# Forming the sums of quarters on GpSimd during the scan steps and storing them, in a kernel of attention and Fourier mixing

## The chip, the core and the metric

The kernel runs on one core of a Trainium2 chip. The metric is the device time of one execution in microseconds. Engines are called by their names: TensorE (PE; its weight loads are PEld), VectorE (DVE), ScalarE (ACT), GpSimd (POOL) and SyncE (SP), which here only issues transfers.

## The reference

```python
x = A_x                                          # 1 x 2048 x 512
g = sigmoid((x * gate_w).sum(-1, keepdims=True))
# a: attention, 32 heads of 16, 2048 queries and keys, softmax, then @ wo
# b: y = dft_seq_re @ (x @ dft_hid_re.T) - dft_seq_im @ (x @ dft_hid_im.T)
return g * a + (1 - g) * b
```

All is float32. The kernel splits each operand of a matmul whose rounding would show into a high part (fp32r) and the rest, and sums three products (high x high, high x low, low x high).

## The kernel before, in words

The work is one long program in an order written out by hand (`tc.manual_schedule()`): every engine has its own stream, in the order in which the Python code emits instructions, and an instruction waits on semaphores for what it needs. SP too takes its transfers in that order. In the built program most of SP's transfers also wait for the one eight places before them in its queue.

The front part projects queries, keys and values, forms the two spectral operands a and b (b is kept in DRAM as `b_d`), multiplies most of the sequence transform (all 16 row blocks of the real part, 0 to 5 of the imaginary part), and scans most of the scores for their row maxima beside it.

Then comes the main loop over `NP * PERIODS` = 512 steps: 16 pairs of heads, 32 steps each (2 halves of the queries by 16 blocks of keys). A half of a pair, 16 steps, is called half pair below. In each step TensorE forms scores (`qk_both`, `qk_single`, L228), ScalarE takes their exponential (L252, L260), and TensorE multiplies with the values (`pv`, L774). At the end of a half pair VectorE copies the sums out (`quotients`, L783), GpSimd spreads the denominators by small transfers (L786), ten steps later `divide` takes reciprocals on VectorE (L792) and lets GpSimd multiply, split and store (L793 to L810).

What stands beside it changes with the step:

- Steps 2 to about 317, the steps with scans: `next_scan` forms one more score block and VectorE reduces it to a maximum (L155).
- From step MIX = 317 on, `fill` gives TensorE six more matmuls in every step: first two row blocks of the spectral part (`spectral`), then, from step HALVED = 349 to 460, the half products (`crosses`), then the output projection (`mix_heads`, `mix_some`). In this part values are multiplied in every second step, for two steps together, so that the pattern repeats every two steps.

The half products replace the last 8 row blocks (rows 1024 to 2047) of the imaginary part, by symmetry. `CROSSES` lists seven products, each of 16 steps. An operand of a product has left parts (2 column blocks f by 2 units u, from `b_d`) and right parts (8 units u, from `ct`). Each is a quarter of its matrix, named (a, b), or a sum or difference of two quarters. `crossed` says at which step, counted from the product's start, each part is formed: from 8 steps before to 7 after. `crossing(r)` calls `begin_unit` (loads the quarters, L948 and L951) 4 steps before, and `form_unit` (L956) on the step: VectorE sums two quarters where there are two (L960), rounds to the high part (L963), and subtracts (L964). The loads go into the ring `craw` of 8 buffers. `gather` takes each finished half product out of the one pair of banks (`pair_banks`) with a copy and an add on VectorE (L1009, L1010), then GpSimd combines it.

The rows that a pair's scores need are loaded on SP: `load_use` for the pair in use (from its 18th step, for the next pair; spread over the steps from MIX on), `load_scan` for a pair to be scanned, and the shifts of the maxima are stored with L190. `load_y` brings in 4 row blocks of the spectral part in one transfer, two of them at step OUT - 25 = 436 and two at step 480. `load_turned` and `output_operands` use the ring `craw` later.

Of the kernel before, what the change touches and what calls it, by code (L numbers as in the profile page):

```python
# [10 lines left out]
F32 = mybir.dt.float32  # L11
# [7 lines left out]
P = 128  # L19
S = 2048  # L20
D = 512
H = 32
DH = 16
NP = H // 2
# [7 lines left out]
PERIODS = 2 * NB  # L32
# [18 lines left out]
OUT = MIX + NB * LATER - SAVED  # L51
# [5 lines left out]
CROSSES = [([((0, 0), 1), ((0, 1), 1)], [((1, 1), 1)]),  # L57
# [6 lines left out]


def build(tc, xT, wqkv, wo, wrT, wiT, cr, ci, ct, gate, out):
    nc = tc.nc
    with ExitStack() as ctx:
        keep = ctx.enter_context(tc.tile_pool(name="keep", bufs=1))
        stk = ctx.enter_context(tc.tile_pool(name="stk", bufs=6))  # L70
# [3 lines left out]
        dram = ctx.enter_context(tc.tile_pool(name="dram", bufs=1, space=DRAM))  # L74
# [7 lines left out]
        b_d = [dram.tile([4, P, D], F32, name=f"b_d{n}") for n in range(NB // 4)]  # L82
# [3 lines left out]
        y_d = [dram.tile([P, 4, D], F32, name=f"y_d{c}") for c in range(NC)]  # L86
# [36 lines left out]
        def load_use(p, spread=False):  # L123
            if p < NP:
                used[p], loads = row_loads(p, nc.sync)
                for load in loads:
                    load()
                    if spread:
                        yield
                qs, ks = used[p]  # L130
                for j in range(2):
                    b = 64 * j + 48
                    nc.sync.dma_start(ks[b:b + 2, :].bitcast(F32), ones_d)
                    for n in range(2):
                        nc.sync.dma_start(qs[b + n:b + n + 1, :].bitcast(F32),
                                          m_d[p][n:n + 1, :, j].rearrange("n g b k -> n b g k"))
# [68 lines left out]
        def block(i):  # L205
            return big.tile([P, 512], F32R, tag=f"b{i}", name=f"b{i}")
# [62 lines left out]
        with ExitStack() as pf:  # L269
# [100 lines left out]
            craw, ready = {}, {}  # L370
# [26 lines left out]
            with ExitStack() as px:  # L397
# [60 lines left out]
                kept = []  # L458
# [68 lines left out]
                raws = [stk.tile([P, S], F32, tag="stk", name="raws") for _ in range(6)]  # L527
# [123 lines left out]
            with ExitStack() as py:  # L651
# [36 lines left out]
                for n, (ph, t, u) in enumerate(coef):  # L688
# [12 lines left out]
                    hi, lo = ready.pop(n)  # L701
# [21 lines left out]
                    for w in range(CS):  # L723
                        s = u * CS + w
# [24 lines left out]
        with ExitStack() as pa:  # L749
            pr = pa.enter_context(tc.tile_pool(name="pr", bufs=1, reuse_waits="tile"))  # L750
            cw = pa.enter_context(tc.tile_pool(name="cw2", bufs=2, reuse_waits="tile"))
            ap = pa.enter_context(tc.tile_pool(name="ap", bufs=1, reuse_waits="tile"))
# [63 lines left out]
            ys, oc = {}, {}  # L816
# [64 lines left out]
                                nc.sync.dma_start(a[i][64 * c + j:64 * c + 64:4, :].bitcast(F32), src[0:DH, j])  # L881
                direct[h].append(a)

            def load_y(c):
                y4 = stk.tile([P, 4, D], F32, tag="stk", name="y4")
                nc.sync.dma_start(y4, y_d[c])
                for t in range(4 * c, 4 * c + 4):
                    ys[t] = y4[:, t % 4, :]

            def take_in(t, ps):  # L890
                nc.vector.scalar_tensor_tensor(ys[t], ps, g[:, t:t + 1], ys[t], op0=ALU.mult, op1=ALU.add)
# [2 lines left out]
            raws, units = [], [(t, u) for t in range(NB - LATER, NB - CROSS) for u in range(NU)]  # L894
            parts = []

            def load_unit():
                if units:
                    t, u = units.pop(0)
                    raw = ap.tile([P, D], F32, tag="craw", name="craw", bufs=8)  # L900
                    raws.append(raw.rearrange("p (c q) -> p c q", q=P))
                    nc.sync.dma_start(raws[-1], ci[t, :, u * CS:(u + 1) * CS, :])
# [28 lines left out]
                nc.sync.dma_start(y_d[t // 4][:, t % 4, :], y)  # L931
                yield

            crossed, begun, sets = [], {}, {}

            for n, (left, right) in enumerate(CROSSES):
                crossed += [(NB * n + at, n, left if f is not None else right, f, u)
                            for at, f, u in ((-8, 0, 0), (-6, None, 0), (-5, None, 1), (-4, None, 2), (-2, 0, 1),
                                             (-1, None, 3), (0, None, 4), (2, None, 5), (3, None, 6), (4, None, 7),
                                             (6, 1, 0), (7, 1, 1))]  # L940

            def begin_unit(at, n, terms, f, u):

                raws = []
                for (a, b), sign in terms:
                    raw = ap.tile([P, 512], F32, tag="craw", name="craw", bufs=8)
                    if f is None:
                        nc.sync.dma_start(raw, ct[8 * a + u, :, 512 * b:512 * b + 512])  # L948
                    else:
                        e = 256 * a + P * f  # L950
                        nc.sync.dma_start(raw.rearrange("p (s e) -> p s e", e=P),  # L951
                                          b_d[2 * b + u][:, :, e:e + P].rearrange("s p e -> p s e"))
                    raws.append(raw)
                begun[at] = raws

            def form_unit(at, n, terms, f, u):  # L956

                raws = begun.pop(at)
                if len(raws) > 1:
                    (nc.vector.tensor_add if terms[1][1] > 0 else nc.vector.tensor_sub)(raws[0], *raws)  # L960
                base = 6 + 2 * u if f is None else 22 * f + 2 * u
                hi, lo = block(base), block(base + 1)
                nc.vector.tensor_copy(hi, raws[0])  # L963
                nc.vector.tensor_sub(lo, raws[0], hi.bitcast(F32))  # L964
                sets[f, u] = hi, lo

            def crossing(r):

                for job in crossed:
                    if job[0] == r + 4:  # L970
                        begin_unit(*job)
                for job in crossed:
                    if job[0] == r:
                        form_unit(*job)
                for job in finishing[:]:
                    if job[0] == r:
                        finishing.remove(job)
                        job[1]()
# [173 lines left out]
            for step in range(NP * PERIODS):  # L1152
                p, i = step // PERIODS, step % PERIODS
                h, kb = i // NB, i % NB
                now[0] = step
                if i == 18:
                    rows = load_use(p + 1, step >= MIX)
                if i >= 18:
                    next(rows, None)
                if step in (MIX - 24, MIX - 20):  # L1160
                    load_unit()
                if step == MIX - 12:
                    split_unit()
                if OUT - 10 <= step < OUT - 4 or step >= OUT + 4:
                    next(operands, None)
                if step in (OUT - 8, OUT + 1):
                    output_rows(int(step > OUT))
                if step in (OUT - 25, (NP - 1) * PERIODS):
                    for c in range(2):
                        load_y(c + 2 * (step > OUT))  # L1170
                if step >= MIX and step % 2 == 0:
                    next(fill)
                if step == 0:
                    pend.append((p, h, kb, ahead[:2]))
                    continue
# [12 lines left out]
                if step >= MIX and step % 2:  # L1188
                    next(fill)
                if step == NP * PERIODS - 1:  # L1190
                    part(3, 0)
                done = None
                for _ in range(min(len(pend), 1) if step < MIX else 0 if step % 2 else 2):
                    done = flush()
                if done and done[2] == NB - 1:
                    halved.append((step + (10 if done[0] < NP - 2 else 7 if done[0] < NP - 1 else 3), quotients(*done[:2])))
                if halved and halved[0][0] <= step:
                    p_, h_ = halved[0][1][:2]
                    divide(*halved.pop(0)[1])
                    if p_ == NP - 2:  # L1200
                        output_rest(h_)
                    if p_ == NP - 2 + (h_ == 0):
                        output_last(h_)
                pend.append((p, h, kb, es))
                crossing(step - HALVED)
                if TURNED <= step < TURNED + CROSS:
                    load_turned(NB - CROSS + step - TURNED)
                if TURNED + 11 <= step < TURNED + 11 + CROSS:
                    take_turned(NB - CROSS + step - TURNED - 11)
# [76 lines left out]
```

## Time and profile before

| | |
|---|---|
| median of 3 runs | 1740.74 us (1738.92 to 1742.15) |
| the profiled execution, own time | 1743.98 us |
| its span | 1742.2 us |
| busy PE / DVE / ACT / POOL | 1709.5 / 1233.7 / 1497.9 / 678.1 us |
| PEld busy | 1033.4 us (59%) |
| loads `craw` from `ct` / from `b_d` in the profile's table of transfers | 96 / 48, 256 KB each |
| sums of quarters on VectorE, L960 | 60, mean 785 ns |
| mean granted TensorE clock | 0.992 |

The span is the time from the first to the last instruction in the trace; the execution's own time is longer by what lies around it. Busy times overlap, and a busy share is an average over parts of the program with different limits. A row of the trace gives start, length, engine, line and tile; in brackets stands how long the engine had been idle and what ended that idle time.

### The profile page before, as it was taken

The page shows a single profiled execution, that of the slowest core. Times are in us where ns is not written, and L with a number is a line of the kernel's source. Part 1 is how long each engine was busy: PE and PEld are TensorE (multiplying, and loading weights), DVE is VectorE, ACT ScalarE, POOL GpSimd, SP SyncE. Part 2 cuts the span into 40 slices and gives each one's busy share as a digit, 9 for nine tenths or more (in the row PEclk, how much of TensorE's full clock was granted, in tenths as well). Part 3 has the DMA queues.
Part 4 walks back from the last instruction along what each step waited for, and adds up shares of the span by engine and source line. Part 5 has one row for each costly group of instructions (what it writes and reads, how often), then busy time and mean ns, then how long its engine had stood idle before and what let it go on. Part 6 is the DMA issues. An engine that isn't in the chain of part 4 may idle for free.

```text
span 1742.2 us, 36286 instructions
## 1 busy us (share of the span) xinstructions
PE 1709.5 (98%) x13560; PEld 1033.4 (59%) x13560; DVE 1233.7 (71%) x2239; ACT 1497.9 (86%) x2472; POOL 678.1 (39%) x789
## 2 busy tenths in 40 slices
PE   9999999999999999999999999999999999979998
PEld 6988888989888884333333333333355544434554
DVE  6898888898999996666666666666715657755343
ACT  6448889888888888999999999999988888767876
POOL 3672436655556661232332324232232232414222
PEclk9999999999999999999999999999999999989999
DMA  7783557444347662232251342434337777787733
GB/s 254 242 279 74 166 152 221 144 117 116 110 114 190 173 126 49 53 77 49 56 102 23 80 78 40 83 58 70 77 92 176 166 193 162 222 198 188 205 99 124
DMA packets 177376, 226.48 MB, mean 130 GB/s; under 512 B 74880, under 2 KB 102000, under 8 KB 170096
## 3 DMA queue, kind: packets, MB, share of 16 engines
q1 hardware_dynamic: 136016, 202.59, 44.7%
q0 software_dynamic: 40608, 20.54, 5.9%
q8 instruction: 106, 1.74, 0.4%
q10 hardware_dynamic: 576, 1.05, 0.2%
q14 instruction: 70, 0.57, 0.1%
HBM read 161.48 MB, written 63.18 MB: 129 GB/s over the span
## 4 chain that ended last, share of the span: by engine, by line
PE 89%; DMA 6%; DVE 3%; issue 1%; ACT 0%; SPq 0%; DVEq 0%; ACTq 0%
PE pvb L774 26%; PE xy L203 25%; PE s L228 17%; PE s L172 9%; PE s L203 7%; PE s L153 5%; DMA craw<-b_d 3%; DMA craw<-ct 2%; DVE craw L960 1%; DVE b L963 0%; DMA raws<-wqkv 0%; DMA q_d<-eh 0%; DMA ks<-kf_d 0%; DVE b L964 0%; PE s L572 0%
## 5 line engine op out<-in xcount | busy, mean ns | idle before, releaser
L252 ACT ACTIVATE eb<-s 128x1024 f32<-128x1024 f32 x512 | 579.4, 1132 | 88.7 <-PE s L228 88.4
L260 ACT ACTIVATE e<-s 128x512 f32<-128x512 f32 x1022 | 608.8, 708 | 0.4 <-PE s L228 0.4
L155 DVE TENSOR_REDUCE mx<-s 128x2 f32<-128x1024 f32 x380 | 461.1, 1225 | 197.2 <-PE s L153 197.0
L774 PE MATMUL pvb<-eb,va 128*17 128x512 f32 x2052 | 516.2, 599 | 0.0
L774 PE MATMUL pvb<-e,va 128*17 128x512 f32 x2044 | 515.3, 599 | 0.0
L178 DVE CUSTOM_DVE_ANT_0 fold<-s,fold 128x512 f32<-128x512 f32 x644 | 433.5, 690 | 56.2 <-PE s L172 29.6
L176 ACT ACTIVATE fold<-s 128x512 f32<-128x512 f32 x644 | 381.9, 604 | 76.2 <-PE s L172 58.0
L228 PEld LDWEIGHTS s<-qs,ks 50*128 50x128 f32 x2048 | 213.9, 185 | 361.8 <-ACT eb L252 268.5
L228 PE MATMUL s<-qs,ks 50*128 50x512 f32 x2048 | 425.3, 437 | 0.0
L203 PE MATMUL xy<-b,c 64*128 64x512 f32 x2448 | 393.6, 392 | 0.1
L172 PE MATMUL s<-ks,qs 48*128 48x512 f32 x1288 | 304.0, 403 | 1.3 <-DVE mx L178 0.9
L203 PEld LDWEIGHTS xy<-b,c 64*128 64x128 f32 x2448 | 283.6, 187 | 17.4 <-issue 1.0
L793 POOL DMA_DIRECT2D r_d<-lc x31 | 18.1, 583 | 443.8 <-DVE lc L792 422.2
L172 PEld LDWEIGHTS s<-ks,qs 48*128 48x128 f32 x1288 | 166.0, 184 | 40.5 <-DVE mx L178 10.8
L774 PEld LDWEIGHTS pvb<-eb,va 128*17 128x17 f32 x2052 | 70.0, 96 | 193.2 <-issue 184.7
L203 PE MATMUL s<-b,b 64*128 64x512 f32 x1050 | 142.2, 400 | 20.2 <-DVE b L1010 18.1
L153 PE MATMUL s<-ks,qs 48*128 48x512 f32 x760 | 158.2, 394 | 0.8 <-DVE mx L155 0.7
L203 PEld LDWEIGHTS s<-b,b 64*128 64x128 f32 x1050 | 101.4, 188 | 47.6 <-DVE b L1010 19.8
L203 PE MATMUL xy<-w,b 64*128 64x512 f32 x768 | 114.6, 392 | 0.0
L383 POOL TENSOR_TENSOR c<-craw,c 128x512 fp32r<-128x512 f32 x84 | 110.4, 1314 | 6.7
L786 POOL DMA_DIRECT2D lc<-ob x124 | 63.8, 521 | 104.3 <-DVE ob L783 103.9
L382 POOL CAST c<-craw 128x512 fp32r<-128x512 f32 x84 | 52.5, 625 | 118.9 <-PE xy L203 116.2
(148 smaller groups left out, 1532.7 us busy)
## 6 DMA issues: line engine op xcount, KB each, us to landing
craw<-ct SPq DMA_DIRECT2D x96, 256.0 KB
qs<-q_d SPq DMA_DIRECT2D x68, 256.0 KB
craw<-cr SPq DMA_DIRECT2D x60, 256.0 KB
craw<-b_d SPq DMA_DIRECT2D x48, 256.0 KB
ks<-k_d SPq DMA_DIRECT2D x46, 256.0 KB
qs<-q_d SPq DMA_DIRECT2D x68, 128.0 KB
craw<-ci SPq DMA_DIRECT2D x32, 256.0 KB
o_d<-oh POOLq DMA_DIRECT2D x30, 256.0 KB, 12.1
```

The source lines that it names most:

```text
L153: nc.tensor.matmul(ps[:, j, :], qs[b:b + 48, qb * P:(qb + 1) * P], ks[b:b + 48, c * 512:(c + 1) * 512], start=True, stop=True)
L155: nc.vector.tensor_reduce(mx[p][:, :, qb, c], ps, axis=AX.X, op=ALU.max)
L172: nc.tensor.matmul(ps, qs[b:b + 48, qb * P:(qb + 1) * P], ks[b:b + 48, c * 512:(c + 1) * 512], start=True, stop=True)
L176: nc.scalar.activation(fold[j], ps, AF.Relu)
L178: nc.vector.tensor_tensor_reduce(out=fold[j], in0=ps, in1=fold[j], scale=1.0, scalar=-3.0e38, op0=ALU.add, op1=ALU.max, accum_out=mx[p][:, ...
L203: nc.tensor.matmul(ps[j], lhs[r], rhs[r], start=first, stop=last)
L228: nc.tensor.matmul(pss[j], ks[b:b + 50, kb * P:(kb + 1) * P], qs[b:b + 50, q0:q0 + 512], start=True, stop=True)
L252: nc.scalar.activation(e, ps, AF.Exp, scale=SCALE)
L260: nc.scalar.activation(e[j], pss[j], AF.Exp, scale=SCALE)
L383: sub(lo, raw, hi.bitcast(F32))
L774: nc.tensor.matmul(pvb[r:r + VC, :], va[:, kb, 2 * p + j, :], es[c][j], start=kb == 0, stop=kb == NB - 1, tile_position=(0, r))
L786: nc.gpsimd.dma_start(lc[32 * n:32 * n + 32, :], ob[r + DH:r + VC, :].rearrange("p (s e) -> p s e", e=16))
```

## The change

The sums of quarters are formed early. `sum_quarters(step - 6)` is called in every step and starts a job every 20 steps: one for each of the 4 left and 8 right parts. A job loads the four quarters (one a step), forms the five sums that the seven products need on GpSimd (L967 of the changed kernel), three steps apart, and stores each in DRAM some 8 steps later (L981, L986). For left parts the products with one term get a plain copy of their quarter, stored likewise; for right parts with one term the quarter is loaded from `ct` as before. The jobs end at about step 250.

`begin_unit` then loads one tile for each part (L1001) and is called 7 steps ahead instead of 4; `form_unit` has no sum any more. `load_y` brings in one row block a call, on 8 steps one after another, instead of 4 in one transfer.

```diff
-            def load_y(c):
-                y4 = stk.tile([P, 4, D], F32, tag="stk", name="y4")
-                nc.sync.dma_start(y4, y_d[c])
-                for t in range(4 * c, 4 * c + 4):
-                    ys[t] = y4[:, t % 4, :]
+            def load_y(t):
+                if t % 4 == 0:
+                    y4 = stk.tile([P, 4, D], F32, tag="stk", name="y4")
+                    for i in range(4):
+                        ys[t + i] = y4[:, i, :]
+                nc.sync.dma_start(ys[t], y_d[t // 4][:, t % 4, :])
...
+            def quarter(f, u, a, b):
+                if f is None:
+                    return ct[8 * a + u, :, 512 * b:512 * b + 512]
+                e = 256 * a + P * f
+                return b_d[2 * b + u][:, :, e:e + P].rearrange("s p e -> p s e")
+
+            def sums_of(f, u):
+                raws = {}
+                for a in range(2):
+                    for b in range(2):
+                        raws[a, b] = ap.tile([P, 512], F32, tag="craw", name="craw", bufs=8)
+                        dst = raws[a, b] if f is None else raws[a, b].rearrange("p (s e) -> p s e", e=P)
+                        nc.sync.dma_start(dst, quarter(f, u, a, b))
+                        yield
+                yield
+                yield
+                store = []
+                for n, cross in enumerate(CROSSES):
+                    terms = cross[f is None]
+                    d = kept[n, f, u] = dram.tile([P, 512], F32, name=f"kept{n}_{f}_{u}")
+                    if len(terms) > 1:
+                        s = ap.tile([P, 512], F32, tag="take", name="sum", bufs=3)
+                        (nc.gpsimd.tensor_add if terms[1][1] > 0 else nc.gpsimd.tensor_sub)(
+                            s, *(raws[k] for k, sign in terms))
+                        store.append((8, d, s))
+                        wait = 3
+                    else:
+                        if f is None:
+                            kept[n, f, u] = quarter(f, u, *terms[0][0])
+                        else:
+                            store.append((1, d, raws[terms[0][0]]))
+                        wait = 0
+                    for _ in range(wait):
+                        yield
+                        store = [(k - 1, d, s) for k, d, s in store]
+                        if store and store[0][0] <= 0:
+                            nc.sync.dma_start(*store.pop(0)[1:])
+                while store:
+                    yield
+                    store = [(k - 1, d, s) for k, d, s in store]
+                    if store[0][0] <= 0:
+                        nc.sync.dma_start(*store.pop(0)[1:])
+
+            summing = []
+
+            def sum_quarters(r):
+                jobs = [(f, u) for f in range(2) for u in range(2)] + [(None, u) for u in range(8)]
+                if r >= 0 and r % 20 == 0 and r // 20 < len(jobs):
+                    summing.append(sums_of(*jobs[r // 20]))
+                for job in summing[:]:
+                    if next(job, summing) is summing:
+                        summing.remove(job)
+
             def begin_unit(at, n, terms, f, u):
-                raws = []
-                for (a, b), sign in terms:
-                    raw = ap.tile([P, 512], F32, tag="craw", name="craw", bufs=8)
...
-                    raws.append(raw)
-                begun[at] = raws
+                begun[at] = ap.tile([P, 512], F32, tag="craw", name="craw", bufs=8)
+                nc.sync.dma_start(begun[at], kept[n, f, u])
 
             def form_unit(at, n, terms, f, u):
-                raws = begun.pop(at)
-                if len(raws) > 1:
-                    (nc.vector.tensor_add if terms[1][1] > 0 else nc.vector.tensor_sub)(raws[0], *raws)
+                raw = begun.pop(at)
...
             def crossing(r):
                 for job in crossed:
-                    if job[0] == r + 4:
+                    if job[0] == r + 7:
                         begin_unit(*job)
...
-                if step in (OUT - 25, (NP - 1) * PERIODS):
-                    for c in range(2):
-                        load_y(c + 2 * (step > OUT))
+                for n, at in enumerate((OUT - 25, (NP - 1) * PERIODS)):
+                    if at <= step < at + 8:
+                        load_y(8 * n + step - at)
...
                 pend.append((p, h, kb, es))
+                sum_quarters(step - 6)
                 crossing(step - HALVED)
```

More of the change, by code (lines that the diff above doesn't have):

```diff
@@ L932, in spectral @@
                 yield
-            crossed, begun, sets = [], {}, {}
+            crossed, begun, sets, kept = [], {}, {}, {}
             for n, (left, right) in enumerate(CROSSES):
@@ L940, in build @@
                                              (6, 1, 0), (7, 1, 1))]
-            def begin_unit(at, n, terms, f, u):
-                raws = []
-                for (a, b), sign in terms:
-                    raw = ap.tile([P, 512], F32, tag="craw", name="craw", bufs=8)
[L947 to L952, printed above, removed]
-                    raws.append(raw)
-                begun[at] = raws
+            def quarter(f, u, a, b):
[3 more added lines that the diff above has]
+                return b_d[2 * b + u][:, :, e:e + P].rearrange("s p e -> p s e")
@@ L956, in form_unit @@
             def form_unit(at, n, terms, f, u):
-                raws = begun.pop(at)
-                if len(raws) > 1:
-                    (nc.vector.tensor_add if terms[1][1] > 0 else nc.vector.tensor_sub)(raws[0], *raws)
+                raw = begun.pop(at)
                 base = 6 + 2 * u if f is None else 22 * f + 2 * u
                 hi, lo = block(base), block(base + 1)
-                nc.vector.tensor_copy(hi, raws[0])
-                nc.vector.tensor_sub(lo, raws[0], hi.bitcast(F32))
+                nc.vector.tensor_copy(hi, raw)
@@ L965, in form_unit @@
+                nc.vector.tensor_sub(lo, raw, hi.bitcast(F32))
                 sets[f, u] = hi, lo
```

## The prediction

> **What bounds the kernel now.** I read the page first, for the time and the chain of work that ended last.
>
> ```profile
> span 1742.2 us, 36286 instructions
> ...
> PE pvb L774 26%; PE xy L203 25%; PE s L228 17%; PE s L172 9%; PE s L203 7%; PE s L153 5%; DMA craw<-b_d 3%; DMA craw<-ct 2%; DVE craw L960 1%; DVE b L963 0%; DMA raws<-wqkv 0%; DMA q_d<-eh 0%; DMA ks<-kf_d 0%; DVE b L964 0%; PE s L572 0%
> ```
>
> Almost the whole chain is TensorE. What is not, is the loads of `craw` from `b_d` and `ct` (the quarters) and the sum of L960 behind them: the very things that the change edits. Next I read that chain in order of time, over the steps after the scans, which hold the half products. The columns are start, length, and what.
>
> ```profile
> 1263.75 1.84 PE pvb L774 x16
> ...
> 1268.12 1.84 PE pvb L774 x16
> ...
> 1373.13 1.89 PE pvb L774 x16
> 1378.37 12.59 DMA craw<-ct
> 1391.03 9.68 DMA craw<-b_d
> ...
> 1407.52 2.01 PE pvb L774 x16
> ...
> 1541.27 13.19 DMA craw<-ct
> ```
>
> After the scans TensorE repeats one pattern every two steps, and the 16 records of L774 mark it: 1268.12 - 1263.75 = 4.37 us a period, and from 1263.75 to 1373.13 the period is 4.375 us if 25 of them lie there. To see where the pattern is broken, I counted the records of L774 by stretches that begin at those marks (in a row: length, PE busy with the count, weight loads with their count, clock, DMA share, GB/s).
>
> ```profile
> 1263.70:1373.10 109.40, 47.78 (x404) 9.20 (x408) 1.00 0.56 139
> 1373.10:1407.50 34.40, 13.39 (x116) 2.59 (x120) 0.96 0.86 170
> 1407.50:1447.00 39.50, 17.32 (x145) 3.26 (x145) 1.00 0.66 181
> 1447.00:1481.90 34.90, 13.39 (x114) 2.57 (x115) 0.97 0.83 184
> 1481.90:1503.60 21.70, 8.88 (x66) 1.59 (x67) 0.90 0.81 218
> 1503.60:1525.40 21.80, 9.54 (x80) 1.82 (x80) 1.00 0.76 220
> 1525.40:1585.90 60.50, 19.43 (x160) 3.68 (x160) 0.89 0.87 207
> ```
>
> The count over 16, cut to whole periods, is 25, 7, 9, 7, 4, 5 and 10. Length minus periods x 4.375 us gives the time lost: 0.0, 3.8, 0.1, 4.3, 4.2, -0.1 and 16.8 us, together **29.1 us**. It holds the slower clock after each stop (0.89 to 0.97 in those rows). The largest loss shows the mechanism.
>
> ```profile
> 1553.58 0.73 PE L228 MATMUL s<-qs,ks 50*128 50x512 f32 x4
> 1567.29 2.93 PE L203 MATMUL s<-b,b 64*128 64x512 f32 x12 [12.97 <-DVE b L1010]
> ...
> 1555.18 0.69 DVE L960 TENSOR_TENSOR craw<-craw 128x512 f32<-128x512 f32 x1 [6.76 <-DMA craw<-ct]
> 1564.03 0.69 DVE L960 TENSOR_TENSOR craw<-craw 128x512 f32<-128x512 f32 x1 [3.97 <-DMA craw<-b_d]
> 1566.54 0.69 DVE L1010 TENSOR_TENSOR b<-s,b 128x512 f32<-128x512 f32 x1
> ```
>
> TensorE has one pair of banks for a half product (pair_banks), so it waits until VectorE has gathered the last one (L1009, L1010). VectorE works in order, and in front of that gather it sits in L960 and waits for quarters. So a late quarter stops TensorE although its own operand isn't due yet.
>
> **The change, part by part.**
>
> Loads in these steps. By CROSSES the seven products need 4 x left terms + 8 x right terms loads: 16, 20, 16, 20, 24, 24, 24 = 144. After, each of 7 x 12 operands is one load: 84, so 60 are gone; the left ones come as whole rows instead of 512 B pieces. They are begun 7 steps ahead of their use instead of 4: at half a period, 2.19 us, a step 7 x 2.19 = 15.3 us instead of 8.75. The longest load pieces in the chain are 12.59 and 13.19 us; 8.75 doesn't cover them, 15.3 does. For demand, two rows, each a stretch in which the operand rows of the next pair (load_use, 14 transfers) are also loaded:
>
> ```profile
> 1296.90:1331.90 35.00, 35.00 (x290) 18.50 (x289) 12.72 (x24) 31.20 (x49) 5.31 (x11) 1.00 0.82 172
> 1366.90:1405.20 38.30, 36.12 (x296) 19.00 (x296) 23.58 (x40) 32.98 (x51) 8.08 (x13) 0.99 0.80 155
> ```
>
> The first stretch carried 13 quarters and 5 other loads of this size with a DMA share of 0.82, and TensorE was busy throughout (35.00 of 35.00), with a lead of 4 steps. After the change a like stretch has 12 a product. The hardest is the one from step 434 on, where load_y adds 8 loads of 256 KB: 20 beside the rows, as in the second stretch, which lost 3.8 us with the short lead; the 6.6 us of added lead cover that. By bytes: from step 434 to 443 come 8 row transfers (1.5 MB), 7 operands (1.8) and 8 pieces of y (2.1), 5.4 MB, in 19.7 us; at the 207 GB/s of the last row above that takes 26 us, a lag of 6.5 us, inside the lead. Value taken: the stalls go but for 2 us (bounds 0 and 13, below).
>
> VectorE in these steps.
>
> ```profile
> L964 DVE TENSOR_TENSOR b<-craw,b 128x512 fp32r<-128x512 f32 x84 | 68.0, 810 | 2.9
> L960 DVE TENSOR_TENSOR craw<-craw 128x512 f32<-128x512 f32 x60 | 47.1, 785 | 47.0 <-DMA craw<-b_d 28.6 <-DMA craw<-ct 18.3
> L963 DVE CAST b<-craw 128x512 fp32r<-128x512 f32 x84 | 43.0, 512 | 9.8 <-DMA craw<-ct 5.4 <-DMA craw<-b_d 1.3
> ```
>
> It loses the 60 sums, 47.1 us of work and 47.0 us of idle time before them. Per product 12 x (0.51 + 0.81) = 15.8 us of forming are left, in 35 us: no new bound. This is not added to the 29.1 us; it is how they go.
>
> What is added in the steps with scans (6 to about 250): 48 loads, 60 GpSimd sums and 68 stores (5 sums for each of 12 operands, 8 plain copies), 116 x 0.262 = 30.4 MB. First, what bounds those steps:
>
> ```profile
> PEld s L228 <- ACT eb L252: 13.6, 16, 0.9
> DVE mx L155 <- PE s L153: 10.5, 16, 0.8
> ...
> 1000.00:1030.00 30.00, 30.00 (x224) 11.32 (x224) 20.12 (x19) 30.00 (x49) 9.37 (x14) 1.00 0.54 89
> ...
> L155 DVE TENSOR_REDUCE mx<-s x285: 1216/1226/1228, 690.0 to 1228.6; 128x2 f32<-128x1024 f32 x143
> L796 POOL TENSOR_TENSOR ob<-ob,rb x17: 1275/1281/1287, 716.4 to 1201.6; 128x512 f32<-128x512 f32 x17
> ```
>
> The first two rows are of the stretch 780 to 810. ScalarE is busy 30.00 of 30.00 us and TensorE's weight loads wait for it each step; a step is (1228.6 - 690.0)/284 = 1.896 us. ScalarE gets no work, so the question is only whether anything added delays a step.
> - GpSimd: 9.37 of 30 us busy. The nearest row for a sum is L796, 1.28 us; 60 x 1.28 = 77 us, some 4 sums or 5.1 us to each half pair of 30.3 us. It stays half idle. In order, a sum can hold up the quotient's work (L786 to L810); that has until the same `ob` buffer is needed again, two half pairs later. Cost 0.
> - VectorE: nothing added. In the build's order the sums start between L786 and L793, where GpSimd waits for a step-paced reciprocal anyway, or after L810.
> - DMA: 30.4 MB in 240 x 1.896 = 455 us is 67 GB/s on top of 89; the sum of 156 lies under the 155 to 220 that the later stretches moved. Cost 0.
> - SP, in order: rows of operands queue behind the stores, which wait for sums, and behind the loads. Here are the issues of two row loads:
>
> ```profile
> 750.66 0.54 SPq L115 DMA_DIRECT2D ks<-k_d  x1
> ...
> 766.33 1.92 SPq L135 DMA_DIRECT2D qs<-m_d  x2
> 779.32 0.56 SPq L115 DMA_DIRECT2D ks<-k_d  x1
> ```
>
> At 779.32 a pair ends and frees its rows, so the pair loaded from 750.66 to 768.3 begins there: 11 us to spare. The one load and one store that the build puts between L190 and this group cost two issues and, at 89 GB/s for 0.52 MB, at most 6 us: hidden. The group issued at 779.32 is now behind stores of sums that follow the divide; The group is due a pair later, 32 steps x 1.896 = 61 us; even if GpSimd came to those sums only with its next step-paced work, half a pair (30 us) later, 30 us would be left for the 18 us of the load. Hidden too. If this cover fails, a late row load stops TensorE four times (every second pair).
>
> [...]
>
> load_y: 16 transfers of 256 KB for 4 of 1 MB, one a step. The last ones (steps 480 to 487) are due from step 485 on, one every two steps: cost 0, at worst the 12 extra issues at 0.56 us (the first row of L115 above), 7 us.
>
> **Sum.** The profiled execution took 1743.98 us: the span and 1.8 us around it. 1743.98 - 29.1 + 2 = 1716.9. The median shown, 1740.74, is 3.2 us lower; the same shift gives **1713.6 us**.
>
> **The rivals.**
>
> *Part of the stalls stays.* The stops of 3.8, 4.3 and 16.8 us end where the rows of a pair interleave with the quarters (DMA share 0.83 to 0.87), and those rows remain, as does y. If these, not the quarters, make the loads late, only the loss of 4.2 us and half of the rest goes: 4.2 + 12.5 = 16.7, so 1724. Against it: the stretch from 1296.9 had the same rows and lost nothing. 0.10.
>
> *The sums hold VectorE up: slower.* The place is L155 in the scan steps.
>
> ```profile
> 1383.00 1.33 POOL L1016 TENSOR_TENSOR b<-b,b 128x512 f32<-128x512 f32 x1 [4.86 <-DVE b L1010]
> ...
> 1383.22 1.66 DVE L964 TENSOR_TENSOR b<-craw,b 128x512 fp32r<-128x512 f32 x1
> ```
>
> Started 0.22 us after a GpSimd sum, L964 took 1.66 instead of its usual 0.69: it ended 0.55 us after the sum, as if it had been held up until it was over. If a sum held a reduction up by its whole 1.28 us, the slack of 10.5/16 = 0.66 us would be used up and 0.62 us lost: 60 x 0.62 = 37 us, more than the 29.1: 1740.7 + 8 + 2 = 1751. It decides from a delay of 0.66 + 29.1/60 = 1.15 us a sum. Against it: 285 reductions took 1216 to 1228 ns, though 17 half pairs put three GpSimd operations each among them. 0.03. [...]
>
> *The queue holds the rows up: slower.* If SP stands so long behind stores that the rows of four pairs come 11 + 8 = 19 us late, each costs 8 us: 1740.7 - 27 + 32 = 1746. For it: everything SP issues waits its turn, and a store waits for GpSimd. Against: the margins above. 0.06.
>
> *The change doesn't do what it says*: the stalls stay whole, 1741, because the gather waits for something else. Only the row [12.97 <-DVE b L1010] with its idle time for `craw` speaks, and it speaks against. 0.03.
>
> **How the numbers follow.** The forecast has 0.78, with its own range 1710 (no stall left, 1711.7, less the 1.8 us from the median to the fastest run of before) to 1720 (8 us left, half of the largest stop). The bound of 13 us for what stays is the second case, 1724. Range 1708 to 1726: 2 us beyond both ends for the scatter of a median; it leaves out the slower cases, no change, and the edge of the second. The measurement can tell about 0.2%, 3.5 us, from no change: faster 0.88 (forecast and first rival), same 0.03, slower 0.09.
>
> **What would show it.** Right: the rows of L774 from the first to the last half product at 4.375 us a period with no stretch over 2 us longer; no idle time "<- DMA craw" on VectorE; clock 0.98 or more there; the reductions still 1.23 us, a scan step still 1.896 us. Wrong: rows "PE s L228" waiting for `ks` or `qs` at pair ends; L155 above 1.3 us; SP waiting on L981 or L986 while TensorE stands; a stop near step 445 with DMA share above 0.85, which would be the first rival.

## The result and the profile after

The changed kernel takes **1719.2 us** (median of 4 runs, 1715.12 to 1722.27) against 1741.45 us before (4 runs, 1738.92 to 1743.03): ratio 0.9872, 95% interval 0.9848 to 0.9896. Its profiled execution took 1719.24 us. First its page: span, busy time by engine, and the chain that ended last.

```profile
span 1717.5 us, 36359 instructions
...
PE 1703.0 (99%) x13560; PEld 1033.1 (60%) x13560; DVE 1189.3 (69%) x2179; ACT 1497.1 (87%) x2472; POOL 751.5 (44%) x849
...
PE pvb L774 27%; PE xy L203 26%; PE s L228 18%; PE s L172 9%; PE s L203 8%; PE s L153 5%; DMA craw<-ct 1%; DMA qs<-q_d 1%; DMA q_d<-eh 0%; DMA raws<-wqkv 0%; DMA raws<-xT 0%; DMA rb<-r_d 0%; PE s L572 0%; DVE y L892 0%; DMA r_d<-lc 0%
```

`craw<-b_d` (3% before) and the sum on VectorE have left the chain. A small new pair is in it: `craw<-ct` and `qs<-q_d`, 1% each. The half products come first: the records of L774 of after, counted by stretches as in the prediction (length, PE busy with the count, weight loads, clock, DMA share, GB/s).

```profile
1267.30:1442.40 175.10, 76.43 (x640) 14.67 (x640) 1.00 0.51 128
1442.40:1473.10 30.70, 13.37 (x112) 2.54 (x112) 1.00 0.73 183
1473.10:1481.90 8.80, 3.82 (x32) 0.73 (x32) 1.00 0.36 84
1481.90:1503.80 21.90, 9.55 (x80) 1.84 (x80) 1.00 0.58 155
1503.80:1530.10 26.30, 11.47 (x96) 2.21 (x96) 1.00 0.66 138
1530.10:1556.30 26.20, 11.47 (x96) 2.21 (x96) 1.00 0.82 195
1556.30:1600.10 43.80, 19.11 (x160) 3.68 (x160) 1.00 0.63 148
```

The counts are 40, 7, 2, 5, 6, 6 and 10 whole periods, 76 in 332.8 us, and 76 x 4.375 = 332.5. Nothing is lost, at clock 1.00 throughout: all 29.1 us of stops are gone. In before VectorE waited 46.9 us for quarters at L960; in after no wait of VectorE for `craw` is left in this part.

But 1743.98 - 29.1 = 1714.9, and the run took 1719.24. The missing 4.3 us show in the copies of L783, one in each half pair: two rows of before, then the same two of after.

```profile
1085.87 0.69 DVE L783 COPY ob<-pvb 128x512 f32<-128x512 f32 x1
1116.18 0.69 DVE L783 COPY ob<-pvb 128x512 f32<-128x512 f32 x1
```

```profile
1086.59 0.69 DVE L783 COPY ob<-pvb 128x512 f32<-128x512 f32 x1
1120.41 0.69 DVE L783 COPY ob<-pvb 128x512 f32<-128x512 f32 x1
```

After runs 0.72 us behind before at 1086 us (0.66 of it stands already at the first copy of the loop, 691.95 against 691.29) and 4.23 us behind at 1120. So there is a new stop of **3.5 us** in the last steps with scans: 1714.9 + 0.7 + 3.5 = 1719.1. To see who made it, read three engines of after over that stretch. GpSimd first, then SP, then TensorE (start, length, engine, line, operation; in brackets the idle time before it and what ended it).

```profile
1075.46 0.57 POOL L793 DMA_DIRECT2D r_d<-lc  x1 [7.07 <-DVE lc L792]
...
1086.09 2.52 POOL L967 TENSOR_TENSOR sum<-craw 128x512 f32<-128x512 f32 x2
...
1113.97 1.28 POOL L967 TENSOR_TENSOR sum<-craw 128x512 f32<-128x512 f32 x1 [22.08 <-DMA craw<-ct]
```

```profile
1067.18 20.55 SPq L981 DMA_DIRECT2D kept_None<-sum  x3
1087.78 1.92 SPq L957 DMA_DIRECT2D craw<-ct  x1
1089.79 1.80 SPq L115 DMA_DIRECT2D ks<-k_d  x1
...
1101.45 0.30 SPq L115 DMA_DIRECT2D qs<-q_d  x1
```

```profile
1111.40 0.47 PE L153 MATMUL s<-ks,qs 48*128 48x512 f32 x1 [1.63 <-DMA qs<-q_d]
```

SP stands from 1067.18 to 1087.73 at three stores of sums. GpSimd works in order too, and it forms the last two of those sums (1086.09) only after the divide's work, which began with L793 at 1075.46, after 7.07 us of waiting for the reciprocals. Behind the stores in SP's queue are the rows of the last pair to be scanned: they begin at 1089.79. In before, this group began here:

```profile
1082.80 0.56 SPq L115 DMA_DIRECT2D ks<-k_d  x1
```

So it is 7 us late, its last piece is issued at 1101.45, and TensorE waits for it until 1111.40. The wait of 1.63 us is not the whole price, since the granted clock fell behind it (after, the first row around the wait, the second the part of it with the lower clock: length, then busy time of PE, PEld, DVE, ACT and POOL, then clock):

```profile
1109.00:1116.00 7.00, 5.37 (x32) 1.76 (x28) 2.79 (x5) 4.35 (x8) 1.80 (x2) 0.76 0.36 129
1112.30:1115.60 3.30, 3.30 (x18) 0.98 (x14) 1.56 (x3) 1.97 (x4) 1.63 (x2) 0.50 0.04 16
```

Over the 3.3 us of the second row the clock is half, and TensorE is busy. 7 x (1 - 0.76) = 1.7 us of clock and 1.63 us of waiting make 3.3 of the 3.5 us.

### The profile page after: what moved, and what is told of

Same layout as the page of the kernel before. It is cut to its first block, busy times and chain, and to the rows that moved or that the text cites. A ratio compares the mean times of both kernels' runs of the same rounds, so it can differ in the third digit from the quotient of the medians.

```text
span 1717.5 us, 36359 instructions
## 1 busy us (share of the span) xinstructions
PE 1703.0 (99%) x13560; PEld 1033.1 (60%) x13560; DVE 1189.3 (69%) x2179; ACT 1497.1 (87%) x2472; POOL 751.5 (44%) x849
## 4 chain that ended last, share of the span: by engine, by line
PE 94%; DMA 3%; DVE 1%; POOL 1%; issue 1%; SPq 1%; ACT 0%; DVEq 0%; POOLq 0%; ACTq 0%
PE pvb L774 27%; PE xy L203 26%; PE s L228 18%; PE s L172 9%; PE s L203 8%; PE s L153 5%; DMA craw<-ct 1%; DMA qs<-q_d 1%; DMA q_d<-eh 0%; DMA raws<-wqkv 0%; DMA raws<-xT 0%; DMA rb<-r_d 0%; PE s L572 0%; DVE y L892 0%; DMA r_d<-lc 0%
## 5 line engine op out<-in xcount | busy, mean ns | idle before, releaser
L155 DVE TENSOR_REDUCE mx<-s 128x2 f32<-128x1024 f32 x380 | 460.9, 1224 | 200.3 <-PE s L153 197.7
L774 PE MATMUL pvb<-eb,va 128*17 128x512 f32 x2052 | 515.3, 598 | 0.0
L774 PE MATMUL pvb<-e,va 128*17 128x512 f32 x2044 | 514.4, 598 | 0.0
L774 PEld LDWEIGHTS pvb<-eb,va 128*17 128x17 f32 x2052 | 69.8, 96 | 190.4 <-issue 181.0
L203 PE MATMUL s<-b,b 64*128 64x512 f32 x1050 | 136.6, 391 | 0.1
L967 POOL TENSOR_TENSOR sum<-craw 128x512 f32<-128x512 f32 x60 | 76.3, 1289 | 114.8 <-DMA kept_None<-sum 51.1
L793 POOL DMA_DIRECT2D r_d<-lc x31 | 18.2, 588 | 220.6 <-DVE lc L792 194.2
```

What stands on the lines that cost most here:

```text
L155: nc.vector.tensor_reduce(mx[p][:, :, qb, c], ps, axis=AX.X, op=ALU.max)
L203: nc.tensor.matmul(ps[j], lhs[r], rhs[r], start=first, stop=last)
L774: nc.tensor.matmul(pvb[r:r + VC, :], va[:, kb, 2 * p + j, :], es[c][j], start=kb == 0, stop=kb == NB - 1, tile_position=(0, r))
L967: (nc.gpsimd.tensor_add if terms[1][1] > 0 else nc.gpsimd.tensor_sub)(s, *(raws[k] for k, sign in terms))
```

## The experiments

My theory had two parts. (A) The 29 us went because 84 transfers arrive through the 8 `craw` buffers in place of 144; the rival causes are the longer lead (7 steps, not 4) and the end of VectorE's sums, which stood ahead of the gather. (B) The new stop comes from SP's order, stores of late sums ahead of rows; the rivals are scatter of the executions and GpSimd disturbing VectorE. Kernels of one group (four rows of the table, in its order) ran on one chip beside before, which took 1742.35, 1743.01 and 1741.83 us there.

| run | median (range), us | ratio to before, 95% |
|---|---|---|
| same_again | 1720.82 (1719.73 to 1721.46) | 0.9882 (0.9868 to 0.9896) |
| rows_first | 1715.56 (1715.25 to 1716.41) | 0.9853 (0.9839 to 0.9867) |
| lead4 | 1720.81 (1715.46 to 1722.82) | 0.9877 (0.9858 to 0.9896) |
| lead7_only | 1735.72 (1734.57 to 1736.33) | 0.9967 (0.9955 to 0.9979) |
| one_quarter | 1715.33 (1714.86 to 1716.91) | 0.9843 (0.983 to 0.9857) |
| no_sum | 1765.24 (1762.27 to 1769.03) | 1.013 (1.0112 to 1.0148) |
| vector_sums | 1766.22 (1763.35 to 1769.44) | 1.0135 (1.0119 to 1.015) |
| lead4_whole_y | 1715.63 (1715.15 to 1716.14) | 0.9844 (0.983 to 0.9857) |
| short_sum | 1733.85 (1730.73 to 1735.04) | 0.9955 (0.9941 to 0.9968) |
| before_rows_first | 1741.13 (1737.95 to 1745.3) | 0.9997 (0.9988 to 1.0007) |
| vector_sums_early | 1748.31 (1746.17 to 1749.12) | 1.0036 (1.0023 to 1.0048) |
| double_sums | 1715.54 (1714.57 to 1717.0) | 0.9853 (0.9837 to 0.9868) |

### The new stop: same_again, rows_first, before_rows_first

**same_again** is the changed kernel once more.

> The changed kernel once more, as the measure for the others of this group. Expected 0.987 of before (0.984 to 0.990), so about 1719 us. Every theory agrees; it also tells whether the one stop that its trace shows in the scan steps (3.5 us at about 1110 us, at the row load of the last pair that is scanned) comes back in another execution: if it does, it belongs to the order of the queue; if not, it was chance.

Its stop came some 28 us later (TensorE starts again at 1140.55, in after at 1111.40), and now VectorE waited first and TensorE for it:

```profile
POOL sum L967 <- DMA craw<-ct: 19.0, 1, 19.0
...
DVE lc L792 <- DMA lc<-ob: 3.6, 1, 3.6
```

Here a sum waited 19.0 us for a quarter that stood behind the row loads in SP's queue; behind that sum GpSimd was late with the transfers of the denominators, and VectorE, in order, waited 3.6 us for them with the reductions behind. It is the same pair of orders, SP's and GpSimd's, each waiting for the other.

**rows_first** asks for the rows of a pair to be scanned four steps earlier, so that they stand ahead of the late stores:

```diff
-                if n + 10 < TOTAL and SEQ[n + 10][0] != SEQ[n + 9][0]:
-                    load_scan(SEQ[n + 10][0])
+                if n + 14 < TOTAL and SEQ[n + 14][0] != SEQ[n + 13][0]:
+                    load_scan(SEQ[n + 14][0])
```

> The changed kernel with the rows of a pair to be scanned asked for 14 steps ahead instead of 10, so that in SP's order they stand before the stores of the two sums which GpSimd forms after its divide work. Theory (queue order): the row load of the last pair starts at about 1083 us, when the buffer comes free, instead of 1089.8, the stop at 1110 us is gone, and the kernel is 3.5 us faster than the changed one, about 1715.5 us. Rival (the load is slow because of the added traffic, whenever it is asked for): the first transfers still take 10 us and more and the stop stays, 1719 us.

It is 5.3 us faster than same_again. SP now begins the rows of the last pair at 1083.64, and the two stores that wait follow at 1091.93:

```profile
1083.64 0.57 SPq L115 DMA_DIRECT2D ks<-k_d  x1
```

Its copies of L783 keep the distance to before through all the scan steps:

```profile
691.76 0.69 DVE L783 COPY ob<-pvb 128x512 f32<-128x512 f32 x1
...
1238.40 0.69 DVE L783 COPY ob<-pvb 128x512 f32<-128x512 f32 x1
```

Before has them at 691.29 and 1237.60: +0.47 and +0.80 us, where the changed kernel went from +0.7 to +4.1. Its four runs lie within 1.2 us, those of the changed kernel within 7 (the fastest, 1715.12, is at the level of rows_first) and those of same_again within 1.7.

**before_rows_first** makes the same edit in the kernel before.

> The kernel before, with the rows of a pair to be scanned asked 14 steps ahead in place of 10, and nothing else. Theory (the stop in the scan steps exists only with the change, whose stores stand ahead of the rows in SP's queue): no difference, ratio 0.998 to 1.002, 1740 to 1745 us. Rival (the earlier rows help either kernel): 3 to 6 us faster, 1735 to 1739 us.

No difference. The four steps are worth something only where stores of sums stand in the queue. (B) is shown: scatter is no rival, since the ranges of rows_first and same_again do not overlap, and the reductions on VectorE keep their length (L155, below).

### The half products: lead4, lead7_only, one_quarter, no_sum, short_sum

**lead4** is the changed kernel with the old lead, **lead7_only** the kernel before with the new one:

```diff
-                    if job[0] == r + 7:
+                    if job[0] == r + 4:
```

> The changed kernel with operands begun 4 steps ahead, as before, instead of 7. Theory (fewer loads are what counts, the lead is a reserve): only the stretch from step 434 on, with the rows of a pair and y beside the operands, loses something: 0 to 6 us over the changed kernel, 1719 to 1725 us. Rival (the lead is what counts, since single loads took 12 to 13 us and 4 steps are 8.75 us): stops come back in all three stretches with row loads, 12 us and more, 1731 us or above.

> The kernel of before, with only its loads of quarters begun 7 steps ahead instead of 4. Rival (the lead is what counts): most of the 29 us go, 1713 to 1720 us. Theory (the number of loads counts, and with 144 of them the ring of 8 buffers, not the call, sets when a load can start): little changes, 1733 to 1743 us.

lead4 is as fast as same_again, and its half products run through without a stop:

```profile
1267.30:1600.10 332.80, 145.23 (x1216) 27.87 (x1216) 1.00 0.57 142
```

lead7_only gets 6 of the 29 us, and the large stop stays. Rows of its L774 stretches:

```profile
1447.70:1480.40 32.70, 13.37 (x112) 2.56 (x112) 1.00 0.89 211
...
1516.90:1567.40 50.50, 16.28 (x128) 3.07 (x128) 0.90 0.81 191
```

32.70 - 7 x 4.375 = 2.1 us and 50.50 - 8 x 4.375 = 15.5 us are still lost. In the first TensorE waits 1.36 us for rows of a pair (`qs<-m_d`), in the second 9.3 us for the gather of L1010. A longer lead through the same 8 buffers can't begin a load before a buffer is free. In lead7_only SP stands at loads whose buffer VectorE hasn't given back (in all, times, longest):

```profile
SPq L948 <- DVE craw L960: 25.1, 15, 8.4
SPq L951 <- DVE craw L960: 14.2, 6, 6.8
```

That is 39.3 us at the sum of L960 alone, where before has 34.5.

**one_quarter** is the kernel before, with 84 loads and with VectorE's sums kept at full length. It leaves out the second quarter of each operand:

```diff
-                for (a, b), sign in terms:
+                for (a, b), sign in terms[:1]:
...
-                if len(raws) > 1:
-                    (nc.vector.tensor_add if terms[1][1] > 0 else nc.vector.tensor_sub)(raws[0], *raws)
+                if len(terms) > 1:
+                    nc.vector.tensor_add(raws[0], raws[0], raws[0])
```

> The kernel before with the first quarter of each operand loaded only: 84 loads in place of 144, asked 4 steps ahead as before; VectorE's 60 sums stay in place and add the quarter to itself, so the second quarter is left out of what is computed, and GpSimd does nothing new. Theory (the stops came from the number of transfers that had to arrive through 8 buffers): the matmuls of the half products run without a stop, 29 us less than the profile before, 1711 to 1717 us. Rival (the stops came from the sums on VectorE, which stand ahead of the gather): 1733 to 1741 us, with the stops at their old places.

The whole gain, with the sums in place: 76 periods run without a stop.

```profile
1265.60:1598.20 332.60, 145.23 (x1216) 27.93 (x1216) 1.00 0.58 142
```

Its waits at L960 (in all, times) are those of two loads, where before had 28.6 and 18.3 us:

```profile
L960 DVE TENSOR_TENSOR craw<-craw x60: 626/684/1789, 1312.6 to 1561.0; 128x512 f32<-128x512 f32 x60
...
  DMA craw<-b_d: 5.7, 2
```

**no_sum** drops the two lines of the sum from the kernel before and keeps the 144 loads, the second quarter unused.

> The kernel before with its 144 loads, but the 60 sums on VectorE are left out, so each operand is its first quarter alone; the second quarter is loaded and not used. Theory (number of transfers): the first quarter of each operand is late nearly as often as the second, so most of the 29 us stay, 1728 to 1741 us; what goes is the share of operands whose second quarter alone was late. Rival (sums): 1711 to 1720 us.

Slower by 22 us, which neither side expected, and for a reason of its own. The queue's waits (in all, times, longest) of no_sum, then of before:

```profile
SPq L948 <- DMA craw<-ct: 84.6, 33, 7.4
```

```profile
SPq L948 <- DMA craw<-ct: 4.7, 9, 1.1
```

A quarter that nobody reads gives its buffer back at once, so the next load into it waits in SP's queue for the transfer before to land. The run says nothing on the sums.

**short_sum** mends it. Each sum is kept but covers one column of 512; the other columns leave the second quarter out:

```diff
-                    (nc.vector.tensor_add if terms[1][1] > 0 else nc.vector.tensor_sub)(raws[0], *raws)
+                    nc.vector.tensor_add(raws[0][:, 0:1], raws[0][:, 0:1], raws[1][:, 0:1])
```

> The kernel before with its 144 loads, each of the 60 sums on VectorE cut to one column of 512 (so all other columns leave the second quarter out); the sum still waits for both quarters and still gives the second buffer back. This mends the run without sums, in which a buffer whose content nobody read was given out again at once, so that the next load waited in SP's queue for the transfer before it to land. Theory (144 transfers through 8 buffers, of which the sum is only the point where lateness shows): the stops stay, at least 20 of 29 us, 1732 to 1743 us. Rival (the 0.7 us of each sum ahead of the gather): 1712 to 1722 us.

8 us faster than before. Its L960 still waits for quarters at least as long as before's (51.8 us to 46.9):

```profile
L960 DVE TENSOR_TENSOR craw<-craw x60: 116/157/1914, 1312.8 to 1576.9; 128x1 f32<-128x1 f32 x60
...
  DMA craw<-ct: 26.7, 12
  DMA craw<-b_d: 25.1, 7
```

What TensorE waits for, in short_sum and then in before (in all, times, longest):

```profile
PE s L203 <- DVE b L1010: 14.5, 4, 12.8
```

```profile
PE s L203 <- DVE b L1010: 18.1, 3, 13.0
```

The large stop stays at its length, and the small ones are nearly gone. So with 144 loads, the length of the sums carries some 8 us of the stops; with 84 it carries nothing. (A) holds in this form: with 84 loads no stop is left, with the old lead (lead4) or with the sums in place (one_quarter); with 144 neither the lead nor the sums' length takes the large stop away. Which property of the 84 loads does it is not shown: fewer transfers, fewer bytes and fewer places taken in the ring came together in every run, and no run gave 144 loads a longer ring. That the left parts come as whole rows isn't needed: one_quarter still loads them in 512 B pieces.

### Where the sums are formed: vector_sums, vector_sums_early, double_sums

**vector_sums** forms the sums in the scan steps on VectorE:

```diff
-                        (nc.gpsimd.tensor_add if terms[1][1] > 0 else nc.gpsimd.tensor_sub)(
+                        (nc.vector.tensor_add if terms[1][1] > 0 else nc.vector.tensor_sub)(
```

> The changed kernel with the sums in the steps with scans formed by VectorE in place of GpSimd. Theory (the stop at 1110 to 1130 us of the changed kernel comes from sums that GpSimd forms late, in its order behind the divide's work, while their stores stand in SP's queue ahead of the rows of the next pair): that stop goes, and the time is 1714 to 1718 us if VectorE, with 60 sums of about 0.7 us, never holds a reduction up. Rival (VectorE works in order, and a sum that waits for its quarter holds up the reduction behind it, and through it the matmuls): 1720 to 1745 us, with VectorE idle for craw ahead of the sums.

The rival held, by more than its bound, though the wait is for another thing. VectorE in one of the stops:

```profile
1028.97 1.23 DVE L155 TENSOR_REDUCE mx<-s 128x2 f32<-128x1024 f32 x1 [0.65 <-PE s L153]
1038.73 0.69 DVE L967 TENSOR_TENSOR sum<-craw 128x512 f32<-128x512 f32 x1 [8.53 <-DMA kept_None<-sum]
1039.34 1.22 DVE L155 TENSOR_REDUCE mx<-s 128x2 f32<-128x1024 f32 x1
```

The sum waits for its own buffer, one of three, which comes free when a store behind the row loads has landed. In after a sum on GpSimd waits 4.64 us for its buffer at 1138 us, and no step is lost there; on VectorE the reduction stands behind the sum, and TensorE behind that. At the end of the scan steps the copy of L783 is 54.5 us behind before's 1237.60; the half products then run without a stop and give 29 back:

```profile
1292.10 0.69 DVE L783 COPY ob<-pvb 128x512 f32<-128x512 f32 x1
```

**vector_sums_early** adds the earlier rows and stores each sum after 4 steps in place of 8 (`store.append((4, d, s))`).

> The changed kernel with the rows 14 steps ahead, the sums on VectorE, and each sum stored 4 steps after it was asked for in place of 8. In the run with VectorE's sums at 8 steps the chain's stops were waits of a sum for its buffer, which a store later in SP's queue gives back, 8.5 us at a time. Theory (the wait in VectorE's order costs, not the sum's 0.69 us): most of those 54 us in the scan steps go, 1714 to 1726 us. Rival (60 sums of 0.69 us are more than VectorE has room for between reductions): still over 1735 us.

Between the two: that copy comes at 1268.48, 30.9 us behind. What is left of the waits for the buffer and for quarters:

```profile
DVE sum L967 <- DMA kept_None<-sum: 16.5, 4, 5.3
...
DVE sum L967 <- DMA craw<-ct: 4.1, 2, 3.9
```

The four waits of 3.9 to 5.3 us fall in four half pairs that take 37.0 to 37.7 us each, where before's take 30.3: 27.9 of the 30.9 us. One half pair with a wait of 1.3 us loses 1.4, and all others together lose some 1.5, though most of them have sums too. So the waits cost, and not the length of the sums. A version on VectorE without such waits was not run.

**double_sums** is rows_first with every sum of GpSimd formed twice into the same buffer. If the 60 further sums held anything up, the time or the reductions on VectorE would show it.

> The changed kernel with the rows asked 14 steps ahead and every sum of GpSimd formed twice into the same buffer, which changes nothing in what is computed: 60 more sums of 1.28 us, GpSimd busy some 830 us in place of 753. [...]

GpSimd was busy for 830.1 us in place of 753.2, and the time is that of rows_first, 1715.54 us against 1715.56. The reductions beside 120 sums:

```profile
L155 DVE TENSOR_REDUCE mx<-s x316: 1164/1227/1228, 658.8 to 1259.8; 128x2 f32<-128x1024 f32 x158
```

### Which parts of the change are needed: lead4_whole_y

It is rows_first with the lead of 4 steps, and with `load_y` as it was before the change (two transfers of 1 MB in one step).

> The changed kernel with the rows of a pair asked 14 steps ahead in place of 10, and with two parts of the change taken back: the loads of the half products are asked 4 steps ahead, and the rows of y are loaded in two whole transfers in one step. Theory (neither part carries anything once there are 84 loads): 1714 to 1717 us, as with the rows asked earlier alone (1715.6). Rival (the split of y or the lead keeps the queue clear): a stop behind the load of y or in the half products, 1719 to 1735 us.

1715.63 us against 1715.56 (ratios to before 0.9844 and 0.9853, with intervals that overlap). Of the change, the sums made in advance and the single loads are all that counts. Rows_first, lead4_whole_y and double_sums are the fastest that compute everything: some 5 us ahead of the changed kernel in same_again, and 26 to 27 us ahead of before.

## Why the prediction was right, and where not

- **Stops of 29.1 us, from late quarters in VectorE's order.** Right in size: without them 76 periods fit in 332.8 us. The cause is right as far as it goes: with 84 loads in place of 144 the stops are gone, lead or sums as before.
- **"The stalls go but for 2 us."** They went whole. The term was 2 us too large.
- **The lead: "8.75 doesn't cover them, 15.3 does."** Wrong as a reason: lead4 has no stop with 8.75 us, and lead7_only keeps most of them with 15.3. With 84 transfers the old lead is enough. The step took the 12.59 and 13.19 us of two pieces of before's chain for a property of a transfer; that they were so long for the number of transfers under way is argued, not shown, since the time of single transfers was not compared.
- **VectorE's sums "are how they go".** Only in part: short_sum gets 8 us by the sum's length alone, one_quarter gets all with the sums kept.
- **GpSimd and VectorE in the scan steps: cost 0.** Right for the sums as such: 60 of them took 1289 ns each (expected 1281), and twice as many cost nothing.
- **SP in the scan steps: "hidden".** This step failed, by 3.5 us in the profile and some 5 in the runs. It tested two groups of `load_use` (those with L135), counted them as loaded when their last issue ended, and gave the second a whole pair, 61 us, until it is due. The group that came late is one of `load_scan`: before begins it at 1082.80, and after's TensorE needs it at 1109.8, some 26 us later, so a delay of 7 us at its start was enough. The two groups of this kind ahead of it began on time (840.74 and 962.13 us in after, 840.02 and 961.41 in before), as no waiting store stood in front of them. The mechanism of the third rival, which had four late groups at 8 us each, is real: one group, 3.5 to 5 us.
- **load_y: cost 0.** Right, either way (lead4_whole_y).
- **Rows and y make the loads late (first rival), or the gather waits for something else (last rival).** Neither: the rows and y are still loaded beside the half products, at a DMA share of up to 0.82, and nothing is lost.
- **The sum.** For the profiled execution it gave 1716.9, which is 2.3 us too low. It kept 2 us of stalls that went, and it lacked the new stop of 3.5 us and the 0.7 us ahead of it: 1716.9 - 2 + 3.5 + 0.7 = 1719.1. That two errors partly cancel is luck. The 3.2 us between the profiled run and the median did not carry over, as after's profiled run equals its median, so the median came out 5.6 us above 1713.6. The measured median lies near the upper end of the forecast's own range, 1720. That end stood for stalls that stay; the time got there by a stop that the forecast had put at nothing.
- **The sums hold VectorE up (second rival).** Refuted where it would have decided. L155 of after, in the main loop's scan steps:

```profile
L155 DVE TENSOR_REDUCE mx<-s x316: 1165/1226/1228, 659.7 to 1264.0; 128x2 f32<-128x1024 f32 x158
```

The median was 1226 ns before, is 1226 now, and is 1227 with 120 sums; the longest took 1228 ns each time. What made L964 of before take 1.66 us at 1383.22 is not shown.
- **The sums on the slower engine.** A sum took 1.9 times as long on GpSimd as on VectorE. The sums of after, then those of vector_sums (shortest, median, longest, ns):

```profile
L967 POOL TENSOR_TENSOR sum<-craw x60: 1266/1289/1303, 671.6 to 1138.5; 128x512 f32<-128x512 f32 x60
```

```profile
L967 DVE TENSOR_TENSOR sum<-craw x60: 627/682/1498, 685.4 to 1175.7; 128x512 f32<-128x512 f32 x60
```

The length of a sum did not decide: the slower engine gave 1715 to 1721 us, the faster one, in its two versions, 1766 and 1748, for what stands behind the sum in each engine's order.

## What to carry to other kernels

When loads through a ring of buffers are late, count the loads before lengthening the lead: here a longer lead through the same ring recovered 6 of 29 us, fewer loads all of them. Work that has slack belongs on the engine whose order has nothing urgent behind it, here one that took 1289 ns for a sum in place of 682; and each store of such work sits in a queue, so look through every urgent load behind it, the last one of the stage too, and ask for those loads ahead of the stores. The scatter of the runs does not tell such a kernel: it was 7 us in the changed kernel and 1.7 in same_again, both with the stop in the trace, and 1.2 in rows_first and 2.4 in double_sums, without it.

## What had not been expected of the hardware

One short stop cost about double, by the granted clock: TensorE waited 1.63 us at 1111 us in after, the clock was 0.50 over the 3.3 us shown above, and 3.5 us were lost. Over whole runs, the same 13560 matmuls kept PE busy for 1700.7 us in rows_first, 1709.5 in before and 1717.0 in vector_sums, at mean clocks of 0.999, 0.992 and 0.986: of the 28 us of span between rows_first and before, 9 are slower matmuls. But a longer wait passed without a lower clock. Before and before_rows_first stop at the same place; first TensorE's wait and the row behind it in before, then in before_rows_first:

```profile
1404.05 2.62 PE L203 MATMUL s<-b,b 64*128 64x512 f32 x12 [2.18 <-DVE b L1010]
...
1404.40:1407.80 3.40, 3.40 (x20) 2.09 (x20) 2.72 (x5) 0.66 (x1) 0.51 (x2) 0.51 0.96 284
```

```profile
1404.30 1.68 PE L203 MATMUL s<-b,b 64*128 64x512 f32 x12 [2.57 <-DVE b L1010]
...
1404.30:1407.70 3.40, 3.40 (x32) 1.88 (x32) 3.13 (x6) 1.45 (x3) 0.86 (x2) 1.00 1.04 271
```

After 2.18 us the clock was 0.51, after 2.57 us it was 1.00. So in these rows the length of the wait alone does not decide it; what does was not tried.
